# Mixing the heads of a linear attention: the order of 32 small products over the four 32-column groups of TensorE's array

## The chip, the cores and the metric

The kernel runs on one core of one Trainium2 chip. The metric is the device time of one execution in microseconds (us), as the median of several timed runs; beside it stands one profiled execution, whose trace gives the rows below. The engines are named as in the profile: PE is TensorE (matmuls), PEld its loading of the left-hand operand, DVE is VectorE, ACT is ScalarE, POOL is GpSimd, SP is SyncE.

## The reference

Three stages: a linear attention with a complex decay, a feed-forward layer with softplus, and four experts whose outputs are weighted per token. The sizes are 2 batches, 8 heads, 768 tokens and 48 features per head, hence 1536 rows of 384 in the two later stages. Only the first stage has to do with the change:

```python
for t in range(S):
    ar, ai = (a_re_n[:, :, t, :, None], a_im_n[:, :, t, :, None])
    new_re = ar * S_re - ai * S_im
    new_im = ar * S_im + ai * S_re
    kv = np.einsum('bhd,bhe->bhde', k[:, :, t], v[:, :, t])
    S_re, S_im = (new_re + kv, new_im)
    y[:, :, t] = np.einsum('bhd,bhde->bhe', q[:, :, t], S_re)
```

Here `a_re_n` and `a_im_n` are the given decays, scaled so that their magnitude is at most about 0.999. Behind it, `h = x @ w_in`, softplus, `@ w_out`, and for each of four experts `relu(x @ w1[e]) @ w2[e]`, weighted and summed.

## The kernel before

**Attention in chunks.** The tokens of a batch are cut into six chunks of 128, and the twelve chunks of both batches are prepared two by two (n = 0 to 5, c = 0 and 1). For a chunk the running product of the decays is taken by prefix sums of phase and logarithm, and query and key are multiplied by its cosine and sine parts, which makes tiles QK of 96 features per head. Six steps follow for each chunk:

- turn(hf), for each half of four heads: transposes of query and key on PE (L510), copied by ACT to qT and kT (L511);
- score(hf): scores of the 128 by 128 tokens of each head (L519), masked by DVE into the tile A (L520);
- mix(): all heads' outputs in one PSUM tile yps of 128 partitions by 3 times 128 tokens. It is the function that changes. A matmul that multiplies zeros opens the tile (L525). A head has 48 output columns: the first 32 go to one of four groups of 32 partitions and to column block 0 or 1, the last 16 (padded to 32, two heads sharing a place) go to column block 2. For both pieces there is a product of the state S with the query (L535; none in the first chunk of a batch, which has no state) and a product of the values v with the scores A (L537). The destination's partitions are also the group of 32 array columns in which the product runs (tile_position);
- state(): products of key and value on three groups in turn (L548), added by DVE to the state (L552, L554);
- done(): yps is copied to X, the input of the next stage, rounded by ACT (L559) and with its remainder by DVE (L560).

**The later stages.** step() runs one block of 128 hidden features: first() with nine products (L226, tile h), an activation, and third() with nine products (L306, tiles y and z) of a block three steps back. There are twelve passes k over 200 such steps. Weights A and B are loaded in fp32 and split into two parts by ACT (L176) and DVE (L177).

**What sets the order.** Each unit of work gets a place on one list (events), sorted by a position given by hand. The attention of the first batch is set before and among the steps of the first passes, that of the second among later passes. When the program is built, the framework fills each engine's queue from that list by its own plan of what is ready when, so units can mix: in the trace of before, products of y stand between those of one mix in the early part. Each queue is worked off in order.

Of the kernel before, what the change touches and what calls it, by code (L numbers as in the profile page):

```python
# [23 lines left out]
P = 128  # L24
B, H, S, D = 2, 8, 768, 48
# [45 lines left out]
def fast_path(ctx: ExitStack, tc, bad, wsc, qkv, a_re, a_im, w_in, w_out, probs, w1, w2, out):  # L71
    nc = tc.nc
# [285 lines left out]
    st_S = [None]  # L358
    st = {}

    def h3(ap):
        return ap.rearrange("p (h e) -> p h e", e=D)
# [103 lines left out]
    def st_out(n):  # L466
        return st["z0"] if n == 0 else (st[n][1], st[n][3])
# [15 lines left out]
    def decay(n, c):  # L483
        qk = st["in", n, c][0]
        lam = st_out(n)[1][:, c, :]
        dec = att.tile([P, 2, HD], F32, tag="dec", name=f"dec{n}_{c}")
        act(dec[:, 0, :], lam, AF.Exp)
        act(dec[:, 1, :], lam, AF.Exp, scale=-1.0)
        nc.vector.scalar_tensor_tensor(flat(qk), flat(dec), DECAY_MAX, flat(qk), ALU.min, ALU.mult)

    def s3_units(n, c):
        b, cc = (CH[n] + c) // CB, (CH[n] + c) % CB
        z = {}

        def prep():
            qk, z["v"] = st.pop(("in", n, c))
            QK = att.tile([P, 2, H, 2 * D], F32, tag="QK", name=f"QK{n}_{c}", bufs=2)
            src = qk.rearrange("p i (h e) -> p i h e", e=D)
            for (t, o) in ((st[n][0], 0), (st_out(n)[0], D)):
                f_ = h3(t[:, c, :]).unsqueeze(1).to_broadcast([P, 2, H, D])  # L500
                nc.vector.tensor_tensor(QK[:, :, :, o:o + D], src, f_, ALU.mult)  # L501
            z["Q"], z["K"] = QK[:, 0], QK[:, 1]

        def turn(hf):
            z["T", hf] = []
            for (src, nm) in ((z["Q"], "q"), (z["K"], "k")):
                dst = att.tile([96, 4, P], F32, tag=nm + "T", name=f"{nm}T{n}_{c}_{hf}", bufs=2)
                tp = psum.tile([P, 4, P], F32, tag="h" if n == 0 else "a", name=f"tp{n}_{c}_{hf}", bufs=2 if n == 0 else 3)
                for hh in range(4):
                    nc.tensor.transpose(tp[:96, hh, :], src[:, hf * 4 + hh, :], ident)  # L510
                nc.scalar.copy(dst, tp[:96])  # L511
                z["T", hf].append(dst)

        def score(hf):
            qT, kT = z["T", hf]
            A = att.tile([P, 4, P], F32, tag="A", name=f"A{n}_{c}_{hf}", bufs=2)
            sp = psum.tile([P, 4, P], F32, tag="a", name=f"sp{n}_{c}_{hf}", bufs=3)
            for hh in range(4):
                nc.tensor.matmul(sp[:, hh, :], kT[:, hh, :], qT[:, hh, :], start=True, stop=True)  # L519
            nc.vector.tensor_tensor(A, sp, tri.unsqueeze(1).to_broadcast([P, 4, P]), ALU.mult)  # L520
            z["A", hf] = A

        def mix():
            yps = psum.tile([P, 512], F32, tag="z" if n < 2 else "a", name=f"yps{n}_{c}", bufs=1 if n < 2 else 3)
            nc.tensor.matmul(yps[:, :3 * P], zrow[0:1, 0:P], zrow[0:1, 0:3 * P], start=True, stop=False,  # L525
                             skip_group_check=True)
            for hf in range(2):
                qT = z["T", hf][0]
                A = z["A", hf]
                for hh in range(4):  # L530
                    hd = hf * 4 + hh
                    for (gg, col, tl) in (((hd % 4) * 32, 0, hd // 4), ((hd // 2) * 32, 32, 2)):
                        dst = yps[gg:gg + 32, tl * P:(tl + 1) * P]
                        if cc > 0:
                            nc.tensor.matmul(dst, st_S[0][:, hd, col:col + 32], qT[:, hh, :], start=False,  # L535
                                             stop=False, tile_position=(0, gg), skip_group_check=True)
                        nc.tensor.matmul(dst, z["v"][:, hd, col:col + 32], A[:, hh, :], start=False,  # L537
                                         stop=(hf == 1), tile_position=(0, gg), skip_group_check=True)
            z["y"] = yps

        def state():
            if cc == CB - 1:
                return
            sps = psum.tile([P, H, VW], F32, tag="a", name=f"sps{n}_{c}", bufs=3)
            K, v = z["K"], z["v"]
            for hd in range(H):
                for gg in range(3):
                    nc.tensor.matmul(sps[32 * gg:32 * gg + 32, hd, :], K[:, hd, 32 * gg:32 * gg + 32],  # L548
                                     v[:, hd, :], start=True, stop=True, tile_position=(0, 32 * gg))
            if cc == 0:  # L550
                st_S[0] = att.tile([96, H, VW], F32, tag="S", name=f"S{b}")
                nc.vector.tensor_copy(st_S[0], sps[:96])  # L552
            else:
                nc.vector.tensor_tensor(st_S[0], sps[:96], st_S[0], ALU.add)  # L554

        def done():
            hi, lo = (XB[b][:, i, :, cc * P:(cc + 1) * P] for i in range(2))
            ysr = z["y"][:, :3 * P].rearrange("p (j t) -> p j t", t=P)
            nc.scalar.copy(hi, ysr)  # L559
            nc.vector.tensor_tensor(lo, ysr, hi.bitcast(F32), ALU.subtract)  # L560

        units = [lambda: (decay(n, c), prep())] if n else [prep]
        return units + [lambda: turn(0), lambda: turn(1), lambda: score(0), lambda: score(1), mix, state, done]

    def excursion(*parts):
# [378 lines left out]
```

## Time and profile before

| | us |
|---|---|
| median of 3 timed runs | 763.38 |
| lowest and highest of them | 762.88, 763.72 |
| span of the profiled execution | 761.7 |
| PE busy in it | 730.5 |
| DVE busy in it | 472.0 |
| ACT busy in it | 432.2 |

The span runs from the first to the last instruction of the profiled execution, for which the trace gives no other time of its own; it is 1.7 us below the median. Matmuls are pipelined, so the duration of one is longer than the distance to the next, and the times at which matmuls start tell more than the durations. A product in fp32 leaves two records on PE and two on PEld.

### The profile page before, as it was taken

What the parts mean: (1) busy time and instruction counts of PE and PEld (TensorE: products, weight loads), DVE (VectorE), ACT (ScalarE), POOL (GpSimd) and SP (SyncE); (2) the same over time, 40 slices, a digit from 0 to 9 for tenths busy, and PEclk for the clock granted to TensorE, in tenths of its full rate; (3) what the DMA queues carried; (4) which work ended last, traced back from release to release, by engine and by line L of the source; (5) the groups of instructions that cost most, each with busy time, mean ns of one, the idle gap of its engine ahead of it and who ended that gap; (6) DMA issues with size and microseconds to landing.
All of it is one profiled execution on the core that took longest, in us unless ns stands there. A gap on an engine that the chain in (4) does not pass through costs nothing.

```text
span 761.7 us, 13007 instructions
## 1 busy us (share of the span) xinstructions
PE 730.5 (96%) x5239; PEld 704.5 (92%) x5239; DVE 472.0 (62%) x812; ACT 432.2 (57%) x756; POOL 31.8 (4%) x31
## 2 busy tenths in 40 slices
PE   2788999999999999999999999999999999999996
PEld 1478899999999999999999999999999999999996
DVE  6999898955639635833742455775855646746631
ACT  7886865888748537623622245665744545446330
POOL 1123000000010110101000000000000000000000
PEclk9699999999999999999999999999999999999998
DMA  7655655631204301410210141230334635626301
GB/s 251 198 166 179 202 156 188 213 120 42 69 15 125 99 1 39 144 55 22 77 63 22 53 124 53 63 104 10 104 115 131 224 104 174 199 84 210 122 31 36
DMA packets 36340, 83.55 MB, mean 110 GB/s; under 512 B 4528, under 2 KB 13232, under 8 KB 36272
## 3 DMA queue, kind: packets, MB, share of 16 engines
q1 hardware_dynamic: 36272, 82.64, 35.1%
q8 instruction: 43, 0.70, 0.4%
q14 instruction: 25, 0.20, 0.1%
HBM read 73.95 MB, written 8.65 MB: 108 GB/s over the span
## 4 chain that ended last, share of the span: by engine, by line
PE 91%; DVE 3%; ACT 2%; DMA 1%; issue 1%; SPq 1%; POOL 0%; POOLq 0%
PE h L226 39%; PE y L306 27%; PE z L306 12%; PE yps L537 3%; PE yps L535 3%; PE sp L519 2%; PE tp L510 2%; PE sps L548 1%; DMA v<-in_qkv_dram 1%; DVE QK L501 1%; DVE im L391 0%; PE pf L429 0%; PE yps L525 0%; PE pl L422 0%; DVE A L177 0%
## 5 line engine op out<-in xcount | busy, mean ns | idle before, releaser
L226 PE MATMUL h<-X,A 128*128 128x384 f32 (+1 forms) x1800 | 341.4, 331 | 1.0 <-DVE A L177 0.8
L226 PEld LDWEIGHTS h<-X,A 128*128 128x128 f32 x1800 | 303.9, 188 | 3.6 <-DVE A L177 1.0
L306 PE MATMUL y<-B,g 128*128 128x384 f32 x768 | 154.2, 335 | 0.0
L249 DVE SCALAR_TENSOR_TENSOR g<-h,g 128x384 fp32r<-128x384 f32 x128 | 71.1, 555 | 117.1 <-ACT g L248 116.6
L248 ACT ACTIVATE g<-h 128x384 fp32r<-128x384 f32 x128 | 62.8, 490 | 140.7 <-PE h L226 109.4
L306 PEld LDWEIGHTS y<-B,g 128*128 128x128 f32 x768 | 134.8, 188 | 1.0 <-ACT chkv L702 0.3
L306 PE MATMUL y<-g,B 128*128 128x384 f32 (+1 forms) x504 | 90.2, 315 | 0.0
L306 PE MATMUL z<-B,g 128*128 128x384 f32 x384 | 87.3, 335 | 0.0
L306 PEld LDWEIGHTS y<-g,B 128*128 128x128 f32 x504 | 78.8, 189 | 1.8 <-issue 0.6
L306 PEld LDWEIGHTS z<-B,g 128*128 128x128 f32 x384 | 68.4, 188 | 0.0
L244 DVE SCALAR_TENSOR_TENSOR e<-h,e 128x384 f32<-128x384 f32 (+1 forms) x60 | 34.9, 581 | 35.1 <-ACT e L97 33.8
L241 ACT ACTIVATE e<-h 128x384 f32<-128x384 f32 (+1 forms) x60 | 30.8, 513 | 41.4 <-PE h L226 38.2
L177 DVE TENSOR_TENSOR A<-rawA,A 128x768 fp32r<-128x768 f32 x40 | 38.5, 964 | 17.9 <-ACT A L176 17.7
L177 DVE TENSOR_TENSOR B<-rawB,B 128x768 fp32r<-128x768 f32 x40 | 38.3, 957 | 10.9 <-ACT B L176 10.8
L176 ACT CAST A<-rawA 128x768 fp32r<-128x768 f32 x40 | 33.1, 828 | 13.0 <-PE z L306 12.5
L97 ACT ACTIVATE e<-e,b_one 128x384 f32<-128x384 f32 (+1 forms) x60 | 38.3, 638 | 1.6
L537 PE MATMUL yps<-A,v 128*32 128x128 f32 x384 | 37.2, 273 | 0.0
L535 PE MATMUL yps<-qT,S 96*32 96x128 f32 x320 | 34.2, 278 | 0.0
L176 ACT CAST B<-rawB 128x768 fp32r<-128x768 f32 x40 | 33.1, 827 | 1.3 <-PE h L226 1.3
L97 ACT ACTIVATE e<-e 128x384 f32<-128x384 f32 (+1 forms) x60 | 32.9, 548 | 1.2
L510 PE MATMUL tp<-ident,QK 128*96 128x128 f32 x192 | 27.2, 288 | 6.1 <-DVE QK L501 5.4
L306 PE MATMUL z<-g,B 128*128 128x384 f32 x144 | 32.7, 335 | 0.0
(148 smaller groups left out, 791.0 us busy)
## 6 DMA issues: line engine op xcount, KB each, us to landing
rawA<-in_w_dram SPq DMA_DIRECT2D x32, 384.0 KB, 3.1
rawB<-in_w_dram SPq DMA_DIRECT2D x32, 384.0 KB, 3.4
rawA<-in_w_in_dram SPq DMA_DIRECT2D x16, 384.0 KB, 3.5
rawB<-in_w_out_dram SPq DMA_DIRECT2D x16, 384.0 KB, 3.7
chkw<-in_w_in_dram SPq DMA_DIRECT2D x16, 384.0 KB, 3.3
chkw<-in_w_out_dram SPq DMA_DIRECT2D x16, 384.0 KB, 3.3
qk<-in_qkv_dram SPq DMA_DIRECT2D x12, 384.0 KB, 3.2
v<-in_qkv_dram SPq DMA_DIRECT2D x12, 256.0 KB, 3.0
```

Source lines behind the costliest of these rows:

```text
L97: i = nc.scalar.activation(out_, in_, fn, **kw)
L176: nc.scalar.copy(hi, src)
L177: nc.vector.tensor_tensor(lo, src, hi.bitcast(F32), ALU.subtract)
L226: nc.tensor.matmul(ps, wt[:, p, kk, o:o + P], XB[b][:, q, kk, tok], start=(n == 0), stop=(n == 3 * KT - 1))
L241: nc.scalar.activation(t, h, AF.Abs)
L244: nc.vector.scalar_tensor_tensor(t, h, 0.0, t, ALU.max, ALU.add)
L248: nc.scalar.activation(g[:, 0, :], h, AF.Relu)
L249: nc.vector.scalar_tensor_tensor(g[:, 1, :], h, 0.0, g[:, 0, :].bitcast(F32), ALU.max, ALU.subtract)
L306: mm = nc.tensor.matmul(ys[j], l_, r_, start=(f == 0 and n == 0 and not mate), stop=(f == FH - 1 and n == 2), skip_group_check=k == 0)
L510: nc.tensor.transpose(tp[:96, hh, :], src[:, hf * 4 + hh, :], ident)
L535: nc.tensor.matmul(dst, st_S[0][:, hd, col:col + 32], qT[:, hh, :], start=False, stop=False, tile_position=(0, gg), skip_group_check=True)
L537: nc.tensor.matmul(dst, z["v"][:, hd, col:col + 32], A[:, hh, :], start=False, stop=(hf == 1), tile_position=(0, gg), skip_group_check=True)
```

## The change

The two loops over heads and the inner order "state product, then score product, for both pieces of a head" are replaced by one list that goes over the groups 0, 1, 2, 3 in turn: the first pieces of heads 0 to 7, then the last pieces of heads 0, 2, 4, 6 and of heads 1, 3, 5, 7. The list is walked twice, first for all state products ("S"), then for all score products ("A"). Products, operands, destinations and groups are the same; which product closes a sum (stop) follows the new order.

```diff
-            for hf in range(2):
-                qT = z["T", hf][0]
-                A = z["A", hf]
-                for hh in range(4):
-                    hd = hf * 4 + hh
-                    for (gg, col, tl) in (((hd % 4) * 32, 0, hd // 4), ((hd // 2) * 32, 32, 2)):
-                        dst = yps[gg:gg + 32, tl * P:(tl + 1) * P]
-                        if cc > 0:
-                            nc.tensor.matmul(dst, st_S[0][:, hd, col:col + 32], qT[:, hh, :], start=False,
-                                             stop=False, tile_position=(0, gg), skip_group_check=True)
-                        nc.tensor.matmul(dst, z["v"][:, hd, col:col + 32], A[:, hh, :], start=False,
-                                         stop=(hf == 1), tile_position=(0, gg), skip_group_check=True)
+            order = ([(hd, (hd % 4) * 32, 0, hd // 4) for hd in range(H)]
+                     + [(hd, (hd // 2) * 32, 32, 2) for hd in (0, 2, 4, 6, 1, 3, 5, 7)])
+            for what in ("S", "A") if cc > 0 else ("A",):
+                for i, (hd, gg, col, tl) in enumerate(order):
+                    hf, hh = hd // 4, hd % 4
+                    dst = yps[gg:gg + 32, tl * P:(tl + 1) * P]
+                    if what == "S":
+                        l_, r_ = st_S[0][:, hd, col:col + 32], z["T", hf][0][:, hh, :]
+                    else:
+                        l_, r_ = z["v"][:, hd, col:col + 32], z["A", hf][:, hh, :]
+                    nc.tensor.matmul(dst, l_, r_, start=False, stop=(what == "A" and not 8 <= i < 12),
+                                     tile_position=(0, gg), skip_group_check=True)
```

## Rows read from the trace of the kernel before

**Rows 1.** The page: busy time, chain that ended last, groups of instructions.

```profile
PE 730.5 (96%) x5239; PEld 704.5 (92%) x5239; DVE 472.0 (62%) x812; ACT 432.2 (57%) x756; POOL 31.8 (4%) x31
...
PE h L226 39%; PE y L306 27%; PE z L306 12%; PE yps L537 3%; PE yps L535 3%; PE sp L519 2%; PE tp L510 2%; PE sps L548 1%; DMA v<-in_qkv_dram 1%; DVE QK L501 1%; DVE im L391 0%; PE pf L429 0%; PE yps L525 0%; PE pl L422 0%; DVE A L177 0%
...
L537 PE MATMUL yps<-A,v 128*32 128x128 f32 x384 | 37.2, 273 | 0.0
L535 PE MATMUL yps<-qT,S 96*32 96x128 f32 x320 | 34.2, 278 | 0.0
```

**Rows 2.** By stretch: length, busy PE, PEld, DVE, ACT, POOL; clock, DMA share, GB/s.

```profile
44.00:88.00 44.00, 40.24 (x517) 34.99 (x516) 39.72 (x70) 32.76 (x58) 8.63 (x5) 1.00 0.55 172
88.00:150.00 62.00, 61.97 (x598) 59.55 (x597) 55.80 (x109) 44.55 (x86) 1.82 (x1) 1.00 0.59 183
...
250.00:435.00 185.00, 185.00 (x1551) 178.12 (x1550) 89.01 (x138) 79.80 (x135) 6.95 (x7) 1.00 0.18 55
435.00:757.00 322.00, 319.70 (x1842) 318.36 (x1840) 189.21 (x326) 163.01 (x287) 0.00 (x0) 1.00 0.37 113
```

**Rows 3.** Timeline of PE, the last mix: start, length, instruction, count of records.

```profile
426.24 0.33 PE L525 MATMUL yps<-zrow 1*128 1x384 bf16 x1
426.50 0.41 PE L535 MATMUL yps<-qT,S 96*32 96x128 f32 x2
426.74 0.38 PE L537 MATMUL yps<-A,v 128*32 128x128 f32 x2
426.96 0.41 PE L535 MATMUL yps<-qT,S 96*32 96x128 f32 x4
427.18 0.41 PE L537 MATMUL yps<-A,v 128*32 128x128 f32 x4
427.40 0.44 PE L535 MATMUL yps<-qT,S 96*32 96x128 f32 x8
427.62 0.44 PE L537 MATMUL yps<-A,v 128*32 128x128 f32 x8
427.89 0.42 PE L535 MATMUL yps<-qT,S 96*32 96x128 f32 x6
...
429.94 0.38 PE L537 MATMUL yps<-A,v 128*32 128x128 f32 x2
430.25 0.44 PE L226 MATMUL h<-X,A 128*128 128x384 f32 x1
```

**Rows 4.** Timeline of PE, the products of state() of one chunk.

```profile
257.06 1.09 PE L548 MATMUL sps<-v,QK 128*32 128x64 f32 x48
258.09 0.44 PE L226 MATMUL h<-X,A 128*128 128x384 f32 x1
```

**Rows 5.** Timeline of PE, the mix of the second batch's first chunk.

```profile
252.23 1.56 PE L537 MATMUL yps<-A,v 128*32 128x128 f32 x32
253.72 0.44 PE L226 MATMUL h<-X,A 128*128 128x384 f32 x1
```

**Rows 6.** Timeline of PE, a mix with state() right behind it.

```profile
323.17 0.40 PE L535 MATMUL yps<-qT,S 96*32 96x128 f32 x2
...
326.39 0.31 PE L548 MATMUL sps<-v,QK 128*32 128x64 f32 x6
...
327.52 0.45 PE L226 MATMUL h<-X,A 128*128 128x384 f32 x1
```

**Rows 7.** Timeline of DVE: in brackets the idle time before, and what ended it.

```profile
50.96 0.56 DVE L560 TENSOR_TENSOR X<-yps,X 128x384 fp32r<-128x384 f32 x1 [1.07 <-ACT X L559]
...
65.51 0.42 DVE L256 TENSOR_REDUCE stats<-gs 128x1 f32<-128x256 f32 x1 [0.85 <-PE gs L254]
...
86.12 0.56 DVE L560 TENSOR_TENSOR X<-yps,X 128x384 fp32r<-128x384 f32 x1 [1.32 <-ACT X L559]
...
108.70 0.56 DVE L560 TENSOR_TENSOR X<-yps,X 128x384 fp32r<-128x384 f32 x1 [1.34 <-ACT X L559]
...
124.58 0.56 DVE L560 TENSOR_TENSOR X<-yps,X 128x384 fp32r<-128x384 f32 x1 [1.23 <-ACT X L559]
```

## Prediction

> **What bounds the kernel now.** I read the page first, then the busy time by stretch, then single mixes on the timeline, then what VectorE (DVE) waited for. A mix is one call of mix(): all products of one chunk of 128 tokens that sum into one yps tile.
>
> The page says that TensorE (PE) is busy for 730.5 of 761.7 us, and that the chain that ended last runs mostly through its products; the two kinds of the mix, L535 (state times query, here S) and L537 (scores times values, here A), have 3% each of it [rows 1]. Their records are 320 and 384: two records for each product, so ten mixes have 16 S and 16 A, and two (the first chunk of each batch) have 16 A alone.
>
> The busy time by stretch tells where a shorter mix is worth its length. From 250 to 435 us, where six of the twelve mixes lie, PE is busy for all of 185.00 us and DVE for 89.01; from there to 757 us PE has 319.70 of 322. Nothing but PE bounds these. From 44 to 88 us PE has 40.24 of 44 and DVE 39.72: neither is full, they wait for each other in turn. From 88 to 150 us PE has 61.97 of 62, with DVE close behind at 55.80 [rows 2]. The clock is 1.00 in all four, the upper level of 2.4 GHz, so no term of the clock enters.
>
> **What a mix does now.** On the timeline of one mix [rows 3] the first product starts at 426.50 and the first instruction after it (h) at 430.25: 3.75 us. Between are 16 rows, S and A in turn, the last at 429.94. Look at the counts: 2, 2, 4, 4, 8, 8, 6, 6, 4, 4, 4, 4, 2, 2, 2, 2 records, 64 in all; and at the starts: they are 0.22 to 0.27 us apart whether a row holds 2 records or 8. A row of 8 is four products, in four groups of 32 columns, at the price of one. So the mix pays for its rows, not for its products.
>
> The counts follow from the order in the program. Head hd goes to group hd mod 4 and its last 16 columns (written hd') to group hd // 2, which gives the groups (hd and hd') 0,0 | 1,0 | 2,1 | 3,1 | 0,2 | 1,2 | 2,3 | 3,3 for heads 0 to 7; every entry is an S and then an A. Suppose that a group holds two products at a time, one S and one A, and that the queue passes nothing that stands behind a product whose group is full. Then the rounds are {0}, {0',1}, {1',2,2',3}, {3',4,4'}, {5,5'}, {6,6'}, {7}, {7'}: 1, 2, 4, 3, 2, 2, 1, 1 products of a kind, which are the counts of the rows, halved. Eight rounds, each an S row and an A row: 16 rows.
>
> **The change, part by part.** It removes no product and adds none: 32 products, their shapes, their sums and the zeroing product before them (L525, 0.26 us to the first S) stay; no DMA is moved and no wait is added. The order alone changes. Each run of four products now covers groups 0, 1, 2, 3: heads 0 to 3, heads 4 to 7, tails 0, 2, 4, 6, tails 1, 3, 5, 7, first for S and then for A.
>
> *A mix with S.* Each group still has 8 products in sequence (4 S and 4 A), and no product stands behind one whose group is full while another is empty. So 8 rows of 8 records instead of 16 rows. The step from a full row to the next is 0.22 (427.40 to 427.62) and 0.27 (427.62 to 427.89) [rows 3], mean 0.245, and the smaller steps are 0.22. From the last row to h there is 0.31 today. The mix becomes 7 x 0.22 + 0.31 = 1.85 us to 7 x 0.245 + 0.31 = 2.03 us, against 3.75: it gives back 1.72 to 1.90 us, and I take 1.81. That products issued in turns share their time is shown by state(), which goes over three groups: 48 records from 257.06 to 258.09, 1.03 us [rows 4]. One after the other they would take 2.6 us by an estimate from the step of a row of 2: 0.22 us [rows 3], so 0.11 a record for 128 columns of the right-hand operand, so 0.055 for the 64 here, 48 times.
>
> *A mix without S.* Its 32 records of A take 252.23 to 253.72, 1.49 us [rows 5]. New: 4 rows, 3 x 0.22 to 3 x 0.245 + 0.31 = 0.97 to 1.05 us. It gives back 0.44 to 0.52. The other such mix, near 38 us, lies before the stretches where PE sets the pace; I count it at nothing.
>
> *A mix with state() right behind it.* From 323.17 the mix runs into the products of state() without a gap: those start at 326.39, beside the last row pair, because group 3 alone is busy then; h starts at 327.52, 4.35 us in all [rows 6]. New: 8 rows of 0.22 to 0.245 are 1.76 to 1.96 us, then state() with its 1.03: 2.79 to 2.99. It gives back 1.36 to 1.56.
>
> *Sum behind 250 us*, where PE is full: four mixes with nothing of state() beside them (at 284.94, 357.56, 392.47 and 426.50, with the same rows), 6.88 to 7.60; the one with state() behind it, 1.36 to 1.56; the one without S, 0.44 to 0.52. Together 8.68 to 9.68; I take 9.2. DVE has 96 us free in that stretch [rows 2], so nothing there becomes the next bound. What could be late next is ScalarE (ACT) and DVE with the copies of yps (L559, L560), and they wait for the mix today.
>
> *From 44 to 88 us*, three mixes. Here DVE is nearly full, and a shorter mix helps only where DVE waited for PE. Three waits of DVE end on what stands behind a mix: 1.07 at 50.96 and 1.32 at 86.12 for the copy of yps, and 0.85 at 65.51 for the sum that PE queues after the mix [rows 7]: 3.24 us. The bounds are nothing (DVE finds no earlier work) and 3 x 1.90 = 5.70 (all of it reaches the end). I take 3.2, the row's own number.
>
> *From 88 to 150 us*, two mixes. PE is full, which speaks for 2 x 1.72 to 2 x 1.90 = 3.44 to 3.80; but DVE has only 6.20 us free in 62 [rows 2], and its waits for these two mixes are 1.34 and 1.23, 2.57 together [rows 7]. Bounds: nothing, if DVE takes the pace over, and 3.80. I take 3.2, between the waits and the full gain.
>
> Sum: 9.2 + 3.2 + 3.2 = 15.6 us. The profiled span of 761.7 becomes 746.1. The median of the timed runs, 763.38, is 1.7 above that span, which I leave as it is: 747.8 us.
>
> **The rivals.**
>
> *DVE takes over before 150 us.* DVE is busy for 90% of both early stretches [rows 2]; a PE that finishes mixes sooner then waits for QK (L501) or for converted weights (L177), and the early mixes give nothing. The time is 763.4 - 9.2 = 754.2. For it: the busy shares. Against it: five of DVE's waits end on a mix.
>
> *The early mixes pay in full.* If DVE's work moves forward with PE's, the sum is 9.68 + 5.70 + 3.80 = 19.2, and the time 744.2. Against it: DVE's free time from 44 to 88 us is only 4.28.
>
> *The products stay in strict order, and nothing changes.* Each product is two records that must follow each other in their group. If no record could start before the one in front of it in the program, then a product in another group could overlap only the second record of the one before: one product each half of 0.22, 32 x 0.11 = 3.52 us, and with the 0.2 to h that is today's 3.75. The time would be 763.4. Against it: the row of 4 at 426.96 holds S of 0' and of head 1, and it starts before the A of 0' (427.18), which stands between them in the program [rows 3]. The Trainium skill, "TensorE: Matmul & The Clock Gate", Part 3, in "What overlaps and what doesn't", says that matmuls keep program order in start and end and only weight loads are pulled ahead; by that rule this change would give next to nothing. The trace of before does not agree: a later product starts 0.2 us before an earlier one.
>
> *Slower: a change of group has a price.* If a group had to be emptied whenever the next product goes to another one, turns over four groups would be the worst order: 32 x 0.22 = 7.04 us and the 0.31, which is 3.6 more than today, ten times, and 16 x 0.22 + 0.31 = 3.83 for those without S, 2.3 more, twice: 40.6 us in all, 804. It decides from the point where a turn costs more than the 0.22 that sharing a row saves. Against it: rows of 8 [rows 3], and state(), which already takes turns over three groups [rows 4]: 48 records in 1.03 us.
>
> **How the numbers follow.** The forecast 0.70; DVE takes over 0.12; early mixes in full 0.11; no change 0.04; slower 0.03. Timed runs lie within 0.1% of their median, so 0.2% (1.5 us) is about what can be told from no change. The first three cases are all faster by more than that: 0.93. The forecast's own span is 745.5 to 751. The range takes in the lower sum, 744.2, and the case with the smaller late sum and no early gain, 763.4 - 8.7 = 754.7: 744.0 to 754.7. It leaves out the last two cases and some of the tails.
>
> **What the profile after would show.** In a mix behind 250 us: 32 records of S and then 32 of A, 1.9 us to the next h, and shares of L535 and L537 in the chain about half of today's. PE still at 100% from 88 us on. ACT's wait for yps shorter by some 1.8 us per mix. In 44 to 88 us PE's idle time grows, ended by QK or converted weights, by what the early term lacks to 5.7. The prediction fails if a group takes fewer than two products (then rows would not fill), if a mix is cut apart by other products where it was whole, or if the planner that fills the queues answers the new order with another order of the early stretch; that last I cannot price from the trace.

## Result and the profile after

The median is 745.61 us (745.51 to 746.25) against 763.5 for the kernel before in the same runs: a ratio of 0.9764, 95% interval 0.975 to 0.9778, so 17.9 us or 2.4% faster. The forecast was 747.8, its range 744.0 to 754.7. The profiled span went from 761.7 to 743.7 us.

On the page of the changed kernel, TensorE (PE) is busy for 18.7 us less, which is more than the span lost; VectorE (DVE) and ScalarE (ACT) do the same work [rows 1]:

```profile
PE 711.8 (96%) x5239; PEld 685.5 (92%) x5239; DVE 471.1 (63%) x812; ACT 432.1 (58%) x756; POOL 30.1 (4%) x31
...
PE 83%; DVE 9%; DMA 2%; ACT 2%; issue 2%; SPq 1%; POOL 0%; DVEq 0%
PE h L226 38%; PE y L306 26%; PE z L306 12%; PE sp L519 2%; PE tp L510 2%; PE yps L537 1%; DVE QK L501 1%; DVE fA L67 1%; DVE im L391 1%; DMA v<-in_qkv_dram 1%; PE sps L548 1%; DVE A L177 1%; DVE qk L489 1%; DMA moe_weights<-fB 1%; DVE fB L66 1%
```

Both kinds of the mix stand on line L537 now, and together have 1% of the chain, which had 3% and 3%. PE's part of the chain fell from 91% to 83%, and DVE's rose from 3% to 9%. Where PE is still the bound and where it no longer is, the busy time by stretch shows (columns as in [rows 2]):

```profile
44.00:88.00 44.00, 40.34 (x555) 34.60 (x554) 42.99 (x78) 37.12 (x64) 6.96 (x5) 1.00 0.60 192
88.00:116.00 28.00, 27.68 (x360) 25.52 (x359) 27.76 (x49) 19.88 (x39) 1.84 (x1) 1.00 0.60 186
116.00:150.00 34.00, 33.91 (x249) 33.05 (x250) 30.71 (x64) 28.34 (x57) 0.00 (x0) 1.00 0.67 219
...
250.00:435.00 185.00, 185.00 (x1540) 179.14 (x1540) 90.22 (x138) 81.81 (x139) 5.93 (x6) 1.00 0.20 64
```

From 250 to 435 us PE has no idle time, as before. From 44 to 88 us DVE went from 39.72 to 42.99 of 44. From 88 to 116 us before was

```profile
88.00:116.00 28.00, 27.97 (x298) 26.55 (x297) 25.73 (x48) 21.64 (x42) 1.82 (x1) 1.00 0.57 173
```

so there DVE went from 25.73 to 27.76 of 28, with PE at 27.68: both are nearly full, and the busy times alone do not tell which of them is the bound. The chain followed within 44 to 116 us speaks for DVE. By line, first after, then before:

```profile
by line: issue 9.6%; DVE QK L501 6.8%; DVE fA L67 6.2%; DVE qk L489 5.0%; DVE A L177 5.0%; DMA rows<-tail 4.5%; DVE A L520 4.3%; DVE fB L66 3.9%; DVE fA L66 3.2%; ACT qT L511 2.9%; ACT kT L511 2.8%; DVE S L554 2.7%; DMA moe_weights<-fA 2.5%
...
by line: PE y L306 14.6%; PE h L226 12.7%; PE yps L537 11.5%; PE yps L535 10.4%; PE sp L519 8.7%; PE tp L510 8.5%; DVE QK L501 6.0%; PE sps L548 3.5%; issue 2.5%; ACT kT L511 2.3%; DVE A L177 1.8%; DVE S L554 1.8%; DVE fB L67 1.7%; ACT qT L
```

After, eight of the lines shown are DVE's, 37.1% together, and none is PE's; before, the first six are PE's.

Three mixes on the timeline of PE, after: the last one, the one without state products, and the one with state() behind it, to be held against [rows 3], [rows 5] and [rows 6].

```profile
244.38 1.08 PE L537 MATMUL yps<-A,v 128*32 128x128 f32 x32
245.39 0.44 PE L226 MATMUL h<-X,A 128*128 128x384 f32 x1
...
312.97 1.08 PE L537 MATMUL yps<-qT,S 96*32 96x128 f32 x32
313.87 1.06 PE L537 MATMUL yps<-A,v 128*32 128x128 f32 x32
314.74 1.07 PE L548 MATMUL sps<-v,QK 128*32 128x64 f32 x48
315.74 0.79 PE L226 MATMUL h<-X,A 128*128 128x384 f32 x3
...
410.73 0.33 PE L525 MATMUL yps<-zrow 1*128 1x384 bf16 x1
411.00 1.08 PE L537 MATMUL yps<-qT,S 96*32 96x128 f32 x32
411.89 1.06 PE L537 MATMUL yps<-A,v 128*32 128x128 f32 x32
412.88 0.62 PE L226 MATMUL h<-X,A 128*128 128x384 f32 x2
```

The last mix takes 1.88 us to the next h (411.00 to 412.88) where it took 3.75; the one without state products 1.01 where it took 1.49; the one with state() 2.77 where the two took 4.35.

These rows also split the gain by place. The mix at 252.23 now starts at 244.38: 7.85 us were won before it. The h at 430.25 now starts at 412.88: 17.37 us, so the six mixes of the second batch gave 9.5. From there to the end of the span another 0.6 us was won (18.0 in all). The instructions of DVE and ACT stay 17.3 us sooner up to 755 us of the kernel before, so it arose in its last 7 us; it is no part of the change that these rows show, and I leave it open.

In the first batch, the marks are DVE's copies of yps:

```profile
50.56 0.54 DVE L560 TENSOR_TENSOR X<-yps,X 128x384 fp32r<-128x384 f32 x1
...
82.11 0.56 DVE L560 TENSOR_TENSOR X<-yps,X 128x384 fp32r<-128x384 f32 x1
...
103.23 0.54 DVE L560 TENSOR_TENSOR X<-yps,X 128x384 fp32r<-128x384 f32 x1
...
117.35 0.55 DVE L560 TENSOR_TENSOR X<-yps,X 128x384 fp32r<-128x384 f32 x1
```

Against [rows 7] they come 0.40, 4.01, 5.47 and 7.23 us sooner, and the idle time in brackets, 1.07 to 1.34 us before each, is gone.

### The profile page after: what moved, and what is told of

Its sections match the earlier page's. It is cut to its first block, busy times and chain, and to the rows that moved or that the text cites. A ratio compares the mean times of both kernels' runs of the same rounds, so it can differ in the third digit from the quotient of the medians.

```text
span 743.7 us, 13006 instructions
## 1 busy us (share of the span) xinstructions
PE 711.8 (96%) x5239; PEld 685.5 (92%) x5239; DVE 471.1 (63%) x812; ACT 432.1 (58%) x756; POOL 30.1 (4%) x31
## 4 chain that ended last, share of the span: by engine, by line
PE 83%; DVE 9%; DMA 2%; ACT 2%; issue 2%; SPq 1%; POOL 0%; DVEq 0%
PE h L226 38%; PE y L306 26%; PE z L306 12%; PE sp L519 2%; PE tp L510 2%; PE yps L537 1%; DVE QK L501 1%; DVE fA L67 1%; DVE im L391 1%; DMA v<-in_qkv_dram 1%; PE sps L548 1%; DVE A L177 1%; DVE qk L489 1%; DMA moe_weights<-fB 1%; DVE fB L66 1%
## 5 line engine op out<-in xcount | busy, mean ns | idle before, releaser
L177 DVE TENSOR_TENSOR A<-rawA,A 128x768 fp32r<-128x768 f32 x40 | 38.5, 963 | 17.8 <-ACT A L176 17.7
L703 DVE TENSOR_REDUCE wmax<-chkv 128x1 f32<-128x384 f32 x32 | 17.6, 549 | 22.2 <-ACT chkv L702 22.2
L701 ACT ACTIVATE chkv<-chkw 128x384 f32<-128x384 int32 x32 | 17.6, 549 | 23.4 <-PE z L306 23.2
```

Of the source, the lines that this page charges most:

```text
L177: nc.vector.tensor_tensor(lo, src, hi.bitcast(F32), ALU.subtract)
L701: nc.scalar.activation(t, raw[:, :, 1], AF.Abs)
L703: nc.vector.tensor_reduce(wmax[:, i:i + 1], t, AX.X, ALU.max)
```

## The experiments

### How many products a group holds

The prediction rests on one reading of [rows 3]: a group holds two products, and the queue passes nothing behind a product whose group is full. A round is the 0.22 us in which each group that holds a product works off one. Three other orders of the same 32 products tell that reading from its rivals; counting rounds gives a price for each beforehand.

**Pairs in turn.** Groups in turn, but each state product is followed at once by its score product:

```diff
-            for what in ("S", "A") if cc > 0 else ("A",):
-                for i, (hd, gg, col, tl) in enumerate(order):
+            for i, (hd, gg, col, tl) in enumerate(order):
+                for what in ("S", "A") if cc > 0 else ("A",):
```

> Groups in turn as in the changed kernel, but each state product is followed at once by the score product of the same piece, as before, so that each group gets two products in a row. Theory (a group takes two products, and the queue stops only behind a full group): the eight rounds stay full, a mix takes 1.9 us as in the changed kernel, and the time is 745 to 747 us. Rival (what helped is that all state products come before all score products): a mix stays near 3.7 us and the time near 763 us. Rival (a group takes one product only): 3.7 us a mix by the same count of rounds, 761 to 764 us.

Measured: 747.87 us, ratio 0.9797 (0.9781 to 0.9813). The last mix, on the timeline of PE:

```profile
414.53 0.45 PE L537 MATMUL yps<-qT,S 96*32 96x128 f32 x8
414.77 0.42 PE L537 MATMUL yps<-A,v 128*32 128x128 f32 x8
414.99 0.44 PE L537 MATMUL yps<-qT,S 96*32 96x128 f32 x8
...
416.49 0.62 PE L226 MATMUL h<-X,A 128*128 128x384 f32 x2
```

Every row is full with 8 records, 0.22 us apart, and the mix takes 1.96 us. So a group does take two products in a row without holding back the next group, and the parting of the two kinds is not what shortens a mix. One product to a group is ruled out. The time is 2.3 us above the changed kernel, just outside the expectation; 0.08 us a mix does not make that. The profiled execution, the slowest of the four (749.82 us; the others 746.96 to 748.34), has it in the early part: DVE's copy of yps is level with the changed kernel's (117.35), but the second batch's first mix starts 3.2 us later (247.59 against 244.38), and between them stands a wait of PE. First the copy, then the wait and the mix:

```profile
117.33 0.55 DVE L560 TENSOR_TENSOR X<-yps,X 128x384 fp32r<-128x384 f32 x1
...
127.62 0.39 PE L254 MATMUL gs<-g,one_r 128*128 128x256 f32 x1 [1.77 <-ACT g L269]
...
247.59 0.32 PE L537 MATMUL yps<-A,v 128*32 128x128 f32 x4
```

Behind the wait comes a stretch at the lower level of the clock (below, the last section). The early queues have another order in this run too, so what made the wait is not shown.

**Four in a row.** State products first, but four for one group before the next:

```diff
+            order.sort(key=lambda o: o[1])
             for what in ("S", "A") if cc > 0 else ("A",):
...
-                    nc.tensor.matmul(dst, l_, r_, start=False, stop=(what == "A" and not 8 <= i < 12),
+                    nc.tensor.matmul(dst, l_, r_, start=False, stop=(what == "A" and i % 4 != 2),
```

> State products first and then score products, as in the changed kernel, but four products in a row for one group before the next group. Theory (two products to a group): of the four, the queue holds the next group back for two, so each change of group costs two products of 0.22 us: 18 x 0.22 = 3.96 us and 0.1 to 0.3, a mix of 4.1 us, a little more than before; the time is 764 to 768 us. Rival (a group takes four or more products, or the queue looks past them): the mix stays at 1.9 us and the time at 746 us. With three to a group it would be 11 x 0.22 = 2.4 us and some 751 us.

Measured: 768.35 us, ratio 1.0074 (1.0057 to 1.0091): slower than the kernel before by 0.7%, and just above the upper end of the expectation (768). The last mix starts at 431.06 and h at 435.32, 4.26 us, where the count gave 3.96 and 0.1 to 0.3:

```profile
431.06 2.13 PE L538 MATMUL yps<-qT,S 96*32 96x128 f32 x29
...
433.28 2.11 PE L538 MATMUL yps<-A,v 128*32 128x128 f32 x29
435.32 0.62 PE L226 MATMUL h<-X,A 128*128 128x384 f32 x2
```

Three products to a group would have made it 2.4, four 1.9.

**Parting alone.** All state products before all score products, the heads in the order of before:

```diff
-            order = ([(hd, (hd % 4) * 32, 0, hd // 4) for hd in range(H)]
-                     + [(hd, (hd // 2) * 32, 32, 2) for hd in (0, 2, 4, 6, 1, 3, 5, 7)])
+            order = [o for hd in range(H) for o in ((hd, (hd % 4) * 32, 0, hd // 4), (hd, (hd // 2) * 32, 32, 2))]
...
-                    nc.tensor.matmul(dst, l_, r_, start=False, stop=(what == "A" and not 8 <= i < 12),
+                    nc.tensor.matmul(dst, l_, r_, start=False, stop=(what == "A" and (tl < 2 or hd % 2 == 1)),
```

> One part of the change alone: all state products before all score products, but within each the heads in the order of before, not the groups in turn. Theory (two products to a group): counting rounds gives 10 steps of 0.22, 2.2 us against 1.76 in turns, so a mix of 2.3 us; ten mixes are 0.4 to 0.5 us longer than in the changed kernel, and the time is 748 to 751 us. So most of the gain comes already from parting the two kinds, because pairs of one group no longer fill it at once. Rival (only the turns matter, the parting does nothing): a mix near 3.7 us and 762 us.

Measured: 750.28 us, ratio 0.9843 (0.9826 to 0.9861). Its last mix takes 2.45 us:

```profile
415.09 1.23 PE L536 MATMUL yps<-qT,S 96*32 96x128 f32 x28
...
417.54 0.44 PE L226 MATMUL h<-X,A 128*128 128x384 f32 x1
```

So either part of the change alone brings most of the gain, in a mix 1.3 us by parting and 1.8 us by turns, and not their sum: both do the same thing, they keep a third product of one group away from a full group. The five orders measured (before 3.75, four in a row 4.26, parting 2.45, pairs in turn 1.96, the change 1.88) stand 0.1 to 0.3 us above the counts for two to a group (3.52, 3.96, 2.20, 1.76, 1.76).

One more rival can be counted in the same way: a queue that looks past a fixed number of waiting products, whatever their groups. The full rows of the pairs (8 rounds) need four or more of them, and with four the order of before would take 14 rounds or fewer, where [rows 3] shows 16. So no such number fits both.

### Where the gain comes from

**The second batch alone**, and **the first batch alone**: the new order under a condition (n >= 3 here, n < 3 in the other kernel), the old one otherwise.

```diff
+            if n >= 3:
...
+            else:
...
```

> The new order in the six mixes of the second batch alone (n of 3 and more), the old order in the first batch. Theory: these lie where TensorE is busy all the time, and each gives back its 1.87 us, those with state() behind it and without state products less: 9.2 to 9.6 us, 754.0 to 754.4 us. Rival (the planner's new order of the queues, not the length of the mix, made part of the gain): more than 0.7 us off that.

Measured: 753.77 us, ratio 0.9877 (0.986 to 0.9893), 9.4 us; 0.2 us below the expected range.

> The new order in the six mixes of the first batch alone (n below 3). Theory: the early stretch gives back 7.9 us, as the marks on VectorE at 226 us show in the changed kernel, and it does so without the late mixes: 755.3 to 756.0 us. The two parts add up to the whole change. Rival (part of it is bought by the late mixes or is lost again behind 250 us): 758 us or more.

Measured: 754.83 us, ratio 0.989 (0.9873 to 0.9906), 8.4 us; 0.5 us below the expected range. The parts add up to 17.8 us of the 18.0: within the noise of the runs, the two stretches are independent.

### What bounds the early part

**More work for DVE, before and after.** Eight masking instructions of the scores are done twice, in n = 1 and 2, in either kernel:

```diff
-            nc.vector.tensor_tensor(A, sp, tri.unsqueeze(1).to_broadcast([P, 4, P]), ALU.mult)
+            for _ in range(2 if 0 < n < 3 else 1):
+                nc.vector.tensor_tensor(A, sp, tri.unsqueeze(1).to_broadcast([P, 4, P]), ALU.mult)
```

> The kernel before, with VectorE's masking of the scores done twice in the four chunks of n = 1 and 2: eight more instructions of 0.60 us, 4.8 us of work that changes no result. Theory (before the change VectorE and TensorE wait for each other there): part of it is taken up by VectorE's idle time, 4.28 us from 44 to 88 and 6.2 us from 88 to 150 us; 1 to 3 us slower, 764.5 to 766.5 us. Rival (VectorE sets the pace already before): 4.8 us, 768.3 us. Rival (TensorE sets it): nothing, 763.5 us.

Measured: 763.57 us, ratio 1.0005 (0.9996 to 1.0015). The extra work (eight steps of 0.60 us, by which DVE's busy time rose from 472.0 to 475.5) cost nothing in the kernel before, less than the theory gave. The kernel before with the extra work, by stretch:

```profile
44.00:88.00 44.00, 41.13 (x527) 36.12 (x526) 40.61 (x73) 33.44 (x58) 7.00 (x5) 1.00 0.53 165
88.00:150.00 62.00, 61.10 (x589) 58.76 (x589) 58.32 (x114) 44.55 (x85) 1.82 (x1) 1.00 0.58 185
```

> The changed kernel with the same eight extra instructions on VectorE. Theory (the shorter mixes have made VectorE the bound from 44 to 116 us, where it is now busy for 98 to 99%): nearly all of the 4.8 us comes out at the end, 4 to 5 us slower than the changed kernel, 749.6 to 750.4 us, and more than in the kernel before. Rival (TensorE still sets the pace there): less than 1.5 us, below 747.1 us.

Measured: 749.94 us, ratio 0.982 (0.9804 to 0.9837), 4.3 us above the changed kernel (3.9 above its second measurement, below). The same work that was free is now paid for. In the profiled execution PE also waits once for longer, and its clock falls behind that. The wait on the timeline of PE:

```profile
92.91 1.32 PE L226 MATMUL h<-X,A 128*128 128x256 f32 x5 [1.99 <-DVE e L244]
```

The busy time by stretch around it, with the clock in the third column from the end:

```profile
89.00:92.90 3.90, 1.93 (x17) 1.72 (x15) 3.90 (x8) 3.90 (x9) 0.00 (x0) 1.00 0.47 141
93.10:96.50 3.40, 3.40 (x17) 3.35 (x17) 3.40 (x8) 2.29 (x5) 0.00 (x0) 0.50 0.84 290
96.50:100.00 3.50, 3.50 (x33) 3.50 (x33) 2.18 (x4) 3.25 (x7) 0.00 (x0) 1.00 0.55 169
```

The slower clock left no lasting loss in that execution. DVE's copy of yps that comes at 82.11 us in the changed kernel comes 3.50 us later here, before that wait and before the clock fell; the second batch's first mix starts 3.52 us later (247.90 against 244.38):

```profile
85.61 0.56 DVE L561 TENSOR_TENSOR X<-yps,X 128x384 fp32r<-128x384 f32 x1
...
247.90 0.32 PE L538 MATMUL yps<-A,v 128*32 128x128 f32 x4
```

So the extra work costs time after and cost none before. The pair does not show it of DVE's time alone: in both runs the extra instructions also gave the early queues another order, as the sequence of ACT's instructions tells from 62 to 65 us on. A further wait of PE, 1.1 us at 697.76, lies far behind the extra work. That DVE is the bound up to 116 us after the change rests on this pair, the busy times and the chain together.

### What is left in a mix

**Without the matmul of zeros** (the first product of each group opens its part of the bank):

```diff
-            nc.tensor.matmul(yps[:, :3 * P], zrow[0:1, 0:P], zrow[0:1, 0:3 * P], start=True, stop=False,
-                             skip_group_check=True)
+            opened = {}
...
-                    nc.tensor.matmul(dst, l_, r_, start=False, stop=(what == "A" and not 8 <= i < 12),
-                                     tile_position=(0, gg), skip_group_check=True)
+                    first = i < 4 and what == ("S" if cc > 0 else "A")
+                    mm = nc.tensor.matmul(dst, l_, r_, start=first, stop=(what == "A" and not 8 <= i < 12),
+                                          tile_position=(0, gg), skip_group_check=True)
+                    if first:
+                        opened[gg] = mm
+                    else:
+                        behind(mm, opened[gg])
```

> The changed kernel without the matmul of zeros that opens the tile: the first product of each group opens its part of the bank instead. The first product started 0.26 to 0.27 us after that matmul in both traces, and that matmul 0.27 us after the last of z. Theory (each of the two steps costs its 0.26): 0.26 us less in each of the twelve mixes, of which nine lie where TensorE sets the pace or nearly so: 2 to 3 us less than the changed kernel, 742.6 to 743.6 us. Rival (the 0.5 us is the price of going from products on the whole array to products in groups, whatever is between): no change, 745.6 us.

Measured: 744.66 us, ratio 0.9753 (0.9737 to 0.9769), between theory and rival; the interval overlaps that of the changed kernel, so the median tells little. The timeline of PE tells more, at the h behind the second batch's first mix and behind its last:

```profile
245.59 0.44 PE L226 MATMUL h<-X,A 128*128 128x384 f32 x1
...
411.81 0.44 PE L226 MATMUL h<-X,A 128*128 128x384 f32 x1
```

The first comes 0.20 us later than in the changed kernel (245.39) and the second 1.07 us sooner (412.88): 1.27 us over five mixes, 0.25 each, as the theory had it where PE is full. The early part gave nothing. The next three runs were made side by side on one chip.

**The changed kernel again, and two versions with a shorter mix.** No matmul of zeros, as above, and state() put right behind mix(); in one version for all mixes, in the other for n >= 3 only.

```diff
-        return units + [lambda: turn(0), lambda: turn(1), lambda: score(0), lambda: score(1), mix, state, done]
+        return units + [lambda: turn(0), lambda: turn(1), lambda: score(0), lambda: score(1), lambda: (mix(), state()), done]
```

> The changed kernel once more, beside the two that follow, for the comparison on one chip: 745 to 746.3 us.

Measured: 746.02 us, ratio 0.9782 (0.9769 to 0.9796).

> The changed kernel, and for the second batch alone (n of 3 and more) no matmul of zeros (the first product of each group opens its part of the bank) and state() put right behind mix() with no step between. Theory (behind 250 us TensorE alone sets the pace, so each saving there reaches the end): 6 x 0.26 = 1.6 us for the zeros; for state() 4 x 0.24, from 2.77 us for a mix with state() behind it against 1.89 and 1.12 apart: 1.0 us. Together 2.6 us less than the changed kernel, 742.6 to 743.4 us. Rival (the planner's order or the later start of h costs as much): 744.5 us or more.

Measured: 743.88 us, ratio 0.9752 (0.9739 to 0.9765): faster than the changed kernel beside it, the intervals apart, by 2.1 us of the 2.6 expected. On the timeline of PE, the products of the mix follow those of z with no matmul of zeros between, and those of state() follow at once:

```profile
311.47 0.69 PE L306 MATMUL z<-B,g 128*128 128x384 f32 x3
312.09 1.08 PE L540 MATMUL yps<-qT,S 96*32 96x128 f32 x32
312.98 1.06 PE L540 MATMUL yps<-A,v 128*32 128x128 f32 x32
313.86 1.07 PE L555 MATMUL sps<-v,QK 128*32 128x64 f32 x48
314.86 0.44 PE L226 MATMUL h<-X,A 128*128 128x384 f32 x1
```

PE is busy there for 184.31 of 185 us: two waits for DVE, 0.4 and 0.3, are new.

> The same two edits in all twelve mixes. Theory (in the first batch VectorE sets the pace to 116 us, so that a shorter mix gives nothing more there): no better than the edits in the second batch alone, 742.5 to 744 us. Rival (TensorE's time still counts there): another 1.5 to 2.5 us less, 740.5 to 741.5 us.

Measured: 748.3 us, ratio 0.9808 (0.9795 to 0.9822). It is slower than with the edits in the second batch alone by 4.4 us; neither theory had that. Without the zeros alone the first batch lost next to nothing (the run before these three), so what goes with the loss is state() joined to the mix there. By DVE's copies of yps, 1.8 us are lost by 83.51 us (81.74 with the edits in the second batch alone) and 3.4 by 251.78 (248.38). Between them PE waits longer for DVE, and the clock falls again; on the timeline

```profile
91.53 1.34 PE L226 MATMUL h<-X,A 128*128 128x256 f32 x9 [2.12 <-DVE e L244]
```

and, by stretch,

```profile
93.00:96.40 3.40, 3.40 (x18) 3.36 (x18) 3.40 (x7) 2.73 (x5) 0.00 (x0) 0.50 0.45 139
```

With state() joined to the mix the early queues have another order too, so how much of the loss is the queues' and how much the clock's stays open. About 1 us more goes with a wait of PE for DVE at 670 us, far behind the mixes.

## Why the prediction held

*What a mix does now* held as put. Two products to a group and a queue that stops behind a full one gave the price of five orders to within 0.3 us, four of them forecast before they ran. The strict order, by which nothing would have changed, falls with the rows: the 32 records of 16 state products start within 0.89 us (411.00 to 411.89), where strict order by records asks 1.76. The prediction priced this rival wrongly, too: its 32 x 0.11 = 3.52 us lets every product overlap the one before it, but in the order of before 20 of the 31 products behind the first go to the same group as the one before them, so that strict order would have taken 20 x 0.22 + 12 x 0.11 = 5.7 us. The 3.75 of [rows 3] spoke against it already, and by it the change would have been a gain. The Trainium skill says in "TensorE: Matmul & The Clock Gate", Part 3, "What overlaps and what doesn't", that matmuls start and end in program order. The trace of before does not agree: a product starts 0.2 us ahead of one that stands before it (426.96 and 427.18 in [rows 3]); in the changed kernel no product has to be passed, so its rows do not test the sentence. The price for a change of group, which would have made the turns the slowest order, is nothing that can be seen: full rows stay 0.22 us apart.

*The terms of a mix* were slightly too careful. A mix with S gave back 1.87 us (1.72 to 1.90, taken 1.81); one without 0.48 (0.44 to 0.52); the one with state() 1.58 (1.36 to 1.56).

*The sum behind 250 us* was taken as 9.2 and came as 9.5 on the rows and 9.4 in the run with these mixes alone.

*The early stretches* are the terms that were mis-sized: 3.2 and 3.2 taken, 7.85 in all measured on the rows and 8.4 in the run by itself, where five mixes of 1.87 would have given 9.35. They make 1.45 of the 2.4 us by which the span fell further than the sum of 15.6; 0.3 came behind 250 us and 0.6 at the very end. So the measured 745.6 us lies nearer to the rival in which the early mixes pay in full (744.2) than to the forecast (747.8). By DVE's copies of yps, 4.0 us were won by 82 us, 3.2 more by 117, and 0.6 more by the start of the next mix at 244 us. The first term stood on the three waits of DVE that end on a mix, 3.24 us. All three are gone, and DVE's idle time from 44 to 88 us fell from 4.28 to 1.01; where the rest of the 4.0 came from is not resolved. The step "neither is full, they wait for each other" gave DVE too much weight for the kernel before: with 4.8 us more work for DVE its time did not move. The second term took 3.2 for fear of DVE, and nearly all of the 3.44 to 3.80 came; a small rest before 44 us or behind 150 us is not resolved.

*DVE takes over before 150 us* came true as a mechanism and not as a price: DVE is busy for 98% of the time from 44 to 116 us and leads the chain there, but most of the early gain had been made by then. A still shorter mix, without the zeros, gained nothing in the first batch.

*The planner*, the term I could not price, hardly answered the change. ACT's 756 instructions stand in the same order in both traces; in DVE's, two instructions moved ahead of a copy of yps (near 51 and 109 us); PE's differ, the mixes' own order aside, only in how the end of a mix and state() mingle. So the gain is that of the shorter mixes. The pairs, the extra work for DVE, the version without zeros and the joined one are other cases: there the early queues changed in many places.

*The signs* came true in part. In the last mix 32 records of each kind follow one another, 1.88 us to the next h. ACT's waits for yps from 250 to 435 us fell from 23.9 to 14.7 us, five of them, so 1.8 each, as put. The share of the mix in the chain fell to a sixth and not to a half, since the early chain went over to DVE. PE's idle time from 44 to 88 us did not grow (3.76 before, 3.66 after), where growth was put.

## What to carry to other kernels

Here fp32 products on different column groups shared TensorE's time as long as the queue met no third product for a group that already held two. Write the order so that any run of products visits all groups, and count rounds to price it; the trace's rows with their record counts show the rounds directly. Then look at which engine is next: where PE was full the shorter mix came out whole (9.5 us), where DVE was near full most of it came out (7.85 of 9.35 us), and there the next shortening gave nothing or, with state() joined to the mix, made the kernel slower.

## What the runs showed that was not expected

The granted clock of PE can fall in the middle of the kernel. In the profiled executions of three runs it stands at 0.50 (1.2 GHz of 2.4) for a stretch right behind a wait of PE: of 1.99 us at 92.91 and of 2.12 us at 91.53 (rows above), and of 1.77 us at 127.62 in the run with pairs in turn, whose busy time by stretch is

```profile
122.00:128.00 6.00, 4.23 (x36) 4.03 (x35) 3.25 (x8) 3.30 (x7) 0.00 (x0) 1.00 0.25 90
128.50:131.90 3.40, 3.40 (x18) 3.40 (x18) 3.33 (x9) 2.48 (x6) 0.00 (x0) 0.50 0.88 274
132.00:136.00 4.00, 4.00 (x36) 4.00 (x35) 2.99 (x7) 2.52 (x5) 0.00 (x0) 1.00 0.62 210
```

18 records of PE in 3.4 us at half the clock, and 36 in 4.0 us behind it. In the changed kernel, whose longest wait of PE from 44 to 150 us is 0.8 us, the clock is 1.00 in all of that stretch. But the length of one wait does not settle it: in the run with the parting alone PE waits for 1.96 us,

```profile
57.18 0.64 PE L510 MATMUL tp<-ident,QK 128*96 128x128 f32 x4 [1.96 <-DVE QK L501]
```

and the clock stays at 1.00 from 44 to 150 us. What else it takes, these runs do not show.
